# Attention and a routed expert layer in one kernel: expert 1's first weight sums one batch earlier, three x sums of the last third in the start-up of the expert units

## The chip, the cores and the metric

The kernel runs on one core of a Trainium2 chip. The metric is the time of one execution in microseconds; a change is judged by the median of several runs. The core's engines are TensorE (PE in the profile; PEld is its weight load), VectorE (DVE), ScalarE (ACT), GpSimd (POOL) and SyncE (SP). VectorE and ScalarE read and write SBUF and PSUM, GpSimd works on SBUF alone here. Each engine takes its own instructions in order and waits for other engines' semaphores.

## The reference

Block-sorted attention for 4 batches, 8 heads, 768 tokens of 64 values, followed by 8 experts whose outputs are all taken, weighted by a balanced routing matrix:

```python
P = sort_net                      # (4, 8, 8, 8); 5 rounds of exp and row/column normalisation
k_sorted = einsum('bhij,bhjcd->bhicd', P, k_b)      # blocks of 96 tokens; v_sorted alike
attn_out = softmax(q_b @ k_sb^T / 8) @ v_sb         # within each block
x = attn_out.transpose(0, 2, 1, 3).reshape(3072, 512)
P = exp(x @ w_gate - max)                           # (3072, 8); 8 rounds of row/column balancing
for e in range(8):
    out += P[:, e:e+1] * (relu(x @ w1[e]) @ w2[e])  # 512 -> 1024 -> 512
```

## The kernel before

**Attention, and expert 0 beside it.** The four batches go through the steps q (query transposes), k (sorted keys), s (scores), m (mixing with the values), t (transposes into xtT), l (routing logits). While batch bb runs, TensorE also computes expert 0 plainly for batch bb - 1 (`expert`: L299 first product, L306 second product). `weave` interleaves the two streams in a fixed order. The loop over bb runs from 1 to 3. In its middle stand the loads of the next batch's v, k and q (`load_batch`, L75, 768 KB each as bf16) and its sorting matrices (`build_r`, L140) on GpSimd, and then the sorting of the next batch's values (`sort_values`, TensorE L152, and sixteenths of the result moved by DMA at L161, half of them issued by GpSimd). In the last batch (bb = 3) this place holds `load_w1(1)` and the sums `sum_w(1)` (L332) instead. GpSimd also copies the queries of batches 2 and 3 (L179) ahead of their transposes.

**Experts 1 to 7.** These use Strassen-like 2x2 products (seven in place of eight), with sums of operands made beforehand. Per expert, `sum_w` makes sums of w1 (8 instructions on GpSimd), `sum_w2` sums of w2 (8 on GpSimd). For x there are three thirds of 1024 tokens; for each, `sum_x` makes four sums (L460): x1 = b12 - b11, x2 = b22 - x1, b12 = b22 - b12 in place, x4 = b21 - x2. The first third's are made by VectorE, unpinned; the second third's by GpSimd; the last third's by VectorE, one a unit from the second unit of chunk 1 on.

The work is cut into chunks (expert, third) of four units each; r counts the units. Unit r does seven first-layer products of chunk r // 4, p1, p5, p6, p2, p7, p3, p4 (`hidden`, L524), interleaved by position j with seven second-layer products q5 to q3 of a pair of token tiles five units back (`Pair`, L635). p7 and p3 end in a ReLU-and-add by VectorE (`relu_sum`, L513), p1, p5 and p6 in a copy by ScalarE, p2 and p4 in a ReLU by ScalarE (L510). p4 adds into the bank that p7's L513 reads. The second-layer banks are read by `gather` (L585, VectorE), which adds them with the routing weight into the output tiles osbl. Before a tile is first added to, `scale0` scales its part from expert 0 by the routing weight (L671, ScalarE). The operands hs of the second layer are made by GpSimd (`sums`, L625), one unit ahead. s (L575 by GpSimd in the first four units, L578 by VectorE later) is c11 - c12.

**The start-up** lies between attention and the units: `last_dense` (T; L692, L700, L704) computes expert 0 for batch 3, and `balance` (C) is the chain that balances the routing matrix: 26 steps, eight rounds of a row step (reduce, add, reciprocal), a column step (multiply, reduce L499) and a step with a matmul (L501) that sums over partitions and three VectorE operations. A string orders the two by hand; the rest of both runs in the first five units (r = 0 to 4), at positions j:

```python
dense, chain, xs = last_dense(), balance(), iter(())
for step in "TTCTTCTTCCTTCCTTTCTT":
    next({"T": dense, "C": chain}[step])
```

**What sets the order.** `pin` puts an instruction behind everything written before it on its engine. TensorE's matmuls are all pinned, and so are most instructions of the expert part. What isn't pinned is placed by a planner that works with costs of its own. `first_x` is a tiny GpSimd copy that reads the last of the first third's x sums; being pinned, it holds what GpSimd does next (expert 1's `sum_w2`, whose weights `load_w2(1)` fetches) until VectorE has made them. `weights(n)` issues n of the queued weight and x sums on GpSimd in each unit.

Of the kernel before, what the change touches and what calls it, by code (L numbers as in the profile page):

```python
# [14 lines left out]
BF16 = mybir.dt.bfloat16  # L15
# [10 lines left out]
def kernel(  # L26
# [11 lines left out]
    nc = tc.nc  # L38
# [25 lines left out]
    pin = tc.keep_in_program_order  # L64
    kt, vt, qt = {}, {}, {}

    def load_batch(bb, parts):
        for d, name in ((vt, "vt"), (kt, "kt"), (qt, "qt")):
            d[bb] = kvp.tile([128, 8, 384], BF16, name=name, bufs=2)
        load_rest(bb, parts)  # L70
# [11 lines left out]
    def load_w1(e):  # L82
        w1t[e] = wp.tile([128, 4, F], BF16, name="w1e")
        pin(nc.gpsimd.dma_start(out=w1t[e],
                                in_=moe_w1[e].rearrange("(kk k) f -> k kk f", k=128)))
# [238 lines left out]
    def sum_w(e):  # L324
        wct[e] = (wcq if e % 2 == 0 else wcp).tile([128, 3, 2, F // 2], BF16, name="wc")
        for kk in range(2):
            a11, a21 = (w1t[e][:, kk, f:f + 512] for f in (0, 512))
            a12, a22 = (w1t[e][:, 2 + kk, f:f + 512] for f in (0, 512))
            s1, s2, s4 = (wct[e][:, j, kk, :] for j in range(3))
            for a, b, o, c in ((a21, a22, ALU.add, s1), (s1, a11, ALU.subtract, s2),  # L330
                               (a11, a21, ALU.subtract, a21), (a12, s2, ALU.subtract, s4)):
                pin(nc.gpsimd.tensor_tensor(out=c, in0=a, in1=b, op=o))  # L332
                yield
# [46 lines left out]
    with ExitStack() as c2:  # L380
        pa = c2.enter_context(tc.tile_pool(name="pa", bufs=8, space=bass.MemoryType.PSUM,
                                           reuse_waits="tile"))
        bank1 = lambda shape, dt: pa.tile(shape, dt, name="bank", tag="bank")
        ebank = lambda: bank1([128, 512], F32)
        for bb in range(1, B):
            ex = expert0(bb - 1, lambda: mps.tile([128, 8, 384], BF16, name="hTs"),
                         ebank, ebank, pin)
            at1, left = attention(bb, bank1), 16 if bb == 1 else 26
            for _ in range(28 - left):
                next(ex)  # L390
            last = 3 if bb + 1 < B else 0
            left -= last
            cut = lambda k: left * k // 12
            weave(at1, ex, 5, cut(5))
            if bb + 1 < B:
                load_batch(bb + 1, [(x, 0, 8) for x in "vkq"])
                build_r(bb + 1, nc.gpsimd, 4)
            else:
                load_w1(1)
                sums = sum_w(1)  # L400
            weave(at1, ex, 3, cut(8) - cut(5))
            if bb + 1 < B:
                weave(sort_values(bb + 1, bank1), ex, 5, last)
            else:
                for _ in sums:
                    pass
            weave(at1, ex, 4, left - cut(8))
            for _ in ex:
                pass
# [6 lines left out]
    mpc, xcp, wq, wcq = late("mpc", 1), late("xcp", 1), late("wq", 2), late("wcq", 1)  # L416
# [36 lines left out]
    xc = xcp.tile([128, 3, 2, N // 2], BF16)  # L453

    def sum_x(p, eng, hold=pin):
        ta, tb = (slice(1024 * p + 512 * i, 1024 * p + 512 * i + 512) for i in range(2))
        b11, b12, b21, b22 = (xtT[:, k:k + 2, t] for k in (0, 2) for t in (ta, tb))
        x1, x2, x4 = (xc[:, j, :, 512 * p:512 * p + 512] for j in range(3))
        for a, b, c in ((b12, b11, x1), (b22, x1, x2), (b22, b12, b12), (b21, x2, x4)):
            hold(eng.tensor_tensor(out=c, in0=a, in1=b, op=ALU.subtract))  # L460
            yield

# [3 lines left out]
    nc.scalar.copy(I128, Ibig)  # L466
    for _ in sum_x(0, nc.vector, lambda ins: ins):
        pass
    first_x = mpc.tile([128, 2], BF16)
    pin(nc.gpsimd.tensor_copy(first_x, xc[:, 2, 0, 0:2]))  # L470

    def balance():

# [195 lines left out]
    def scale0(ts):  # L669
        for t in ts:  # L670
            pin(nc.scalar.activation(out=osbl[:, t, :], in_=osbl[:, t, :], func=AF.Copy,  # L671
                                     scale=glog[:, t, 0:1]))

    def last_dense():

        at = [0]

        def two_banks():
            at[0] += 1
            return rings["oacc"][at[0] % 2]  # L680

        for c in range(2):
            c0 = (B - 1) * S + c * 384
            if c == 0:
                h = [hTb[1][:, fb, 0:384] for fb in range(8)]
            else:
                two = [hsp.tile([128, 4, 384], BF16, name="hs") for _ in range(2)]
                h = [two[fb // 4][:, fb % 4, :] for fb in range(8)]
            for fb in range(8):
                hps = (rings["bk"][(0, 2, 3)[fb % 3]] if c == 0 else two_banks())[:, 0:384]  # L690
                for kk in range(4):
                    pin(nc.tensor.matmul(hps, w1t[0][:, kk, fb * 128:(fb + 1) * 128],  # L692
                                         xtT[:, kk, c0:c0 + 384],
                                         start=(kk == 0), stop=(kk == 3)))
                pin(relu(h[fb], hps))
                yield
            for tt in range(3):
                oacc = rings["bk"][(1, 4)[tt]] if c == 0 and tt < 2 else two_banks()
                for fb in range(8):
                    pin(nc.tensor.matmul(oacc, h[fb][:, tt * 128:(tt + 1) * 128],  # L700
                                         w2t[0][:, fb, :], start=(fb == 0), stop=(fb == 7)))
                    if fb == 3:
                        yield
                pin(nc.scalar.copy(osbl[:, c0 // 128 + tt, :], oacc))  # L704
                yield

    dense, chain, xs = last_dense(), balance(), iter(())
    for step in "TTCTTCTTCCTTCCTTTCTT":
        next({"T": dense, "C": chain}[step])

    queue = [sum_w2(1), sum_x(1, nc.gpsimd)]

    def weights(n):
# [6 lines left out]
    C = 3 * (E - 1)  # L720
# [4 lines left out]
    for m, o in enumerate(ends):  # L725
        e, p, hT, _ = chunks[-1]
# [4 lines left out]
    for r in range(len(pairs) + 6):  # L731
        n, i = r // 4, r % 4
        if n < C:
            e, p, hT, s3 = chunks[n]
            if i == 0 and (n == 1 or n > 1 and p == 0) and e + 1 < E:
                load_w1(e + 1)
                queue.append(sum_w(e + 1))
            if r == 8 or p == 1 and i == 2 and n > 1 and e + 1 < E:
                load_w2(2 if r == 8 else e + 1)
                queue.append(sum_w2(2 if r == 8 else e + 1))  # L740
            steps, rest = hidden(e, p, i, hT, s3, r < 4)
        else:
            steps, spares, rest = spares[:7], spares[7:], None
        if r == 5:
            xs = sum_x(2, nc.vector)
        k = r - 5
        if k + 1 in range(len(pairs)):
            pairs[k + 1].sums()
        weights((0, 2, 2, 0, 0)[r] if r < 5 else 4 if r < 8 else 1 + i % 2)
        now = pairs[k] if k in range(len(pairs)) else None  # L750
        if r < 5:
            outs = [lambda: next(dense), None, lambda: next(dense), None,
                    lambda: next(dense)]
        else:
            outs = [getattr(a, b) for a, b in
                    ((now, "q5"), (before, "q7"), (now, "q1"), (before, "q4"),
                     (now, "q6"), (now, "q2"), (now, "q3")) if a]
        if r == 5:
            for _ in chain:
                pass  # L760
            scale0([0, 4])
        for j in range(max(len(steps), len(outs))):
            if j < len(steps):
                steps[j]()
                if j == 3 and n < C:
                    if k + 1 in range(1, 12):
                        scale0([8 * ((k + 1) // 4) + (k + 1) % 4 + 4 * m for m in range(2)])
                    if k + 1 in range(len(pairs)):
                        pairs[k + 1].keep()
            if j < len(outs) and outs[j]:  # L770
                outs[j]()
            if r < 5 and j < 6 and (6 * r + j) % 4 != 3:
                next(chain, 0)
            if j == 1 and late:
                late()
                late = None
            if j == 3:
                next(xs, 0)
        late, before = rest, now
        if n >= C and not spares and not before:  # L780
            break
# [30 lines left out]
```

## Time and profile before

| | |
|---|---|
| median of 3 runs | 680.86 us (680.52 to 681.43) |
| profiled execution | 680.97 us, span 679.2 us |
| mean granted TensorE clock | 0.998 |
| TensorE busy | 659.0 us (97%) |
| VectorE busy | 474.8 us (70%) |
| ScalarE busy | 380.5 us (56%) |
| GpSimd busy | 473.6 us (70%) |

In the timeline a row gives the start, the time to the end of the group, the engine, the source line, the operation with its output and input tiles, and in brackets the idle time ahead of it and what ended it. In lists of waits the numbers are the total, the number of waits and the longest. In lists of DMA issues the last number is the time in us from issue to landing. Times are counted from the span's start.

The span falls into attention of batch 0 and its loads (0 to 49 us), attention of batches 1 to 3 with expert 0 beside it (49 to 135 us), the start-up (135 to 146 us) and the units (from 146 us).

### The profile page before, as it was taken

What the parts mean: (1) busy time and instruction counts of PE and PEld (TensorE: products, weight loads), DVE (VectorE), ACT (ScalarE), POOL (GpSimd) and SP (SyncE); (2) the same over time, 40 slices, a digit from 0 to 9 for tenths busy, and PEclk for the clock granted to TensorE, in tenths of its full rate; (3) what the DMA queues carried; (4) which work ended last, traced back from release to release, by engine and by line L of the source; (5) the groups of instructions that cost most, each with busy time, mean ns of one, the idle gap of its engine ahead of it and who ended that gap; (6) DMA issues with size and microseconds to landing.
All of it is one profiled execution on the core that took longest, in us unless ns stands there. A gap on an engine that the chain in (4) does not pass through costs nothing.

```text
span 679.2 us, 13352 instructions
## 1 busy us (share of the span) xinstructions
PE 659.0 (97%) x5136; PEld 434.1 (64%) x5136; DVE 474.8 (70%) x977; ACT 380.5 (56%) x737; POOL 473.6 (70%) x439
## 2 busy tenths in 40 slices
PE   4989999999999999999999999999999999999997
PEld 2656666554566666666666666666666666666665
DVE  6727556758587777777777777777777777777775
ACT  3757646356767765455555555555555555555540
POOL 4542324474979998959697988879796979836641
PEclk9999999999999999999999999999999999999999
DMA  9898843402140304030403030020303040000224
GB/s 146 168 217 127 139 82 63 63 1 37 28 62 2 63 1 63 1 63 1 63 1 63 1 50 14 12 52 3 61 1 63 1 63 1 1 0 32 94 84 167
DMA packets 31905, 36.58 MB, mean 54 GB/s; under 512 B 2016, under 2 KB 24288, under 8 KB 31840
## 3 DMA queue, kind: packets, MB, share of 16 engines
q0 software_dynamic: 26400, 27.82, 25.8%
q1 hardware_dynamic: 5440, 7.90, 3.4%
q8 instruction: 40, 0.66, 0.4%
q14 instruction: 25, 0.20, 0.1%
HBM read 52.45 MB, written 6.29 MB: 86 GB/s over the span
## 4 chain that ended last, share of the span: by engine, by line
PE 88%; DVE 5%; DMA 4%; issue 1%; ACT 1%; POOL 1%; SPq 0%; DVEq 0%; POOLq 0%
PE oacc L635 36%; PE bk L524 36%; PE bank L299 4%; PE bank L306 3%; DMA qt<-in_q_dram 3%; PE bank L232 1%; PE bk L601 1%; PE oacc L700 1%; PE bk L692 1%; DMA vsb<-vs 1%; PE bank L215 1%; PE bank L196 1%; PE bank L243 1%; DVE xc L460 1%; PE bk L700 1%
## 5 line engine op out<-in xcount | busy, mean ns | idle before, releaser
L585 DVE SCALAR_TENSOR_TENSOR osbl<-oacc,glog,osbl 128x256 f32<-128x256 f32 (+1 forms) x410 | 219.4, 536 | 127.7 <-PE oacc L635 117.8
L510 ACT ACTIVATE hT<-bk 128x512 bf16<-128x512 f32 (+1 forms) x176 | 104.2, 592 | 151.8 <-PE bk L524 131.9
L524 PE MATMUL bk<-xtT,w1e 128*128 128x512 bf16 x504 | 149.1, 379 | 0.0
L635 PEld LDWEIGHTS <-hs 128*128 128x128 bf16 x984 | 96.3, 98 | 63.0 <-issue 0.3
L635 PEld LDWEIGHTS <-hT 128*128 128x128 bf16 x904 | 88.4, 98 | 59.6 <-issue 2.4
L625 POOL TENSOR_TENSOR hs<-hT 128x512 bf16<-128x512 bf16 x82 | 94.7, 1155 | 38.3 <-DVE hT L513 28.6
L635 PE MATMUL oacc<-w2e,hT 128*128 128x256 bf16 x764 | 114.6, 273 | 1.1 <-DVE osbl L585 1.1
L625 POOL TENSOR_TENSOR hs<-hT,hs 128x512 bf16<-128x512 bf16 x82 | 95.1, 1159 | 6.4
L625 POOL TENSOR_TENSOR hs<-hs,hT 128x512 bf16<-128x512 bf16 x82 | 95.1, 1159 | 6.4
L524 PE MATMUL bk<-xc,wc 128*128 128x512 bf16 x336 | 99.1, 379 | 0.0
L635 PE MATMUL oacc<-w2e,hs 128*128 128x256 bf16 x616 | 92.4, 273 | 0.0
L524 PEld LDWEIGHTS <-w1e 128*128 128x128 bf16 x672 | 65.7, 98 | 14.9 <-issue 3.6
L559 ACT COPY p<-bk 128x512 f32<-128x512 f32 x84 | 49.1, 585 | 23.9 <-PE bk L524 23.8
L513 DVE CUSTOM_DVE_ANT_0 hT<-bk,p 128x512 bf16<-128x512 f32 x84 | 57.9, 690 | 6.6 <-PE bk L524 1.9
L553 ACT COPY u<-bk 128x512 f32<-128x512 f32 x84 | 49.2, 586 | 22.2 <-PE bk L524 22.1
L544 ACT COPY bk<-bk 128x512 f32<-128x512 f32 x84 | 48.0, 571 | 20.5 <-PE bk L524 20.5
L513 DVE CUSTOM_DVE_ANT_0 hT<-bk,u 128x512 bf16<-128x512 f32 x84 | 57.2, 681 | 0.6 <-PE bk L524 0.6
L635 PE MATMUL oacc<-w2s,hs 128*128 128x256 bf16 x368 | 55.2, 273 | 0.0
L578 DVE SCALAR_TENSOR_TENSOR s<-bk,hT 128x512 bf16<-128x512 f32 x80 | 54.5, 681 | 0.0
L524 PEld LDWEIGHTS <-wc 128*128 128x128 bf16 x504 | 49.4, 99 | 7.5
L524 PE MATMUL bk<-xc,w1e 128*128 128x512 bf16 x168 | 49.9, 379 | 1.9 <-DVE hT L513 1.8
L524 PE MATMUL bk<-xtT,wc 128*128 128x512 bf16 x168 | 50.0, 379 | 0.0
(129 smaller groups left out, 858.5 us busy)
## 6 DMA issues: line engine op xcount, KB each, us to landing
w1e<-in_moe_w_dram POOLq DMA_DIRECT2D x8, 1024.0 KB, 8.1
w2e<-in_moe_w_dram POOLq DMA_DIRECT2D x8, 1024.0 KB, 8.9
out_dram<-osbl SPq DMA_DIRECT2D x23, 256.0 KB, 2.0
vt<-in_v_dram POOLq DMA_DIRECT2D x3, 768.0 KB, 10.5
vsb<-vs SPq DMA_DIRECT2D x16, 97.5 KB, 4.8
vsb<-vs POOLq DMA_DIRECT2D x16, 97.5 KB, 4.4
qt<-in_q_dram POOLq DMA_DIRECT2D x4, 384.0 KB, 12.8
kt<-in_k_dram POOLq DMA_DIRECT2D x4, 384.0 KB, 13.3
```

The source lines that it names most:

```text
L299: hold(nc.tensor.matmul(hps[:, 0:n], w1t[e][:, kk, fb * 128:(fb + 1) * 128], xtT[:, kk, c0:c0 + n], start=(kk == 0), stop=(kk == 3)))
L306: hold(nc.tensor.matmul(oacc, hTs[:, fb, tt * 128:(tt + 1) * 128], w2t[e][:, fb, :], start=(fb == 0), stop=(fb == 7)))
L510: relu = lambda o, x: nc.scalar.activation(out=o, in_=x, func=AF.Relu)
L513: return nc.vector._custom_dve(TENSOR_ADD_SAT, out=o, in0=x, in1=y, s0=TOP, s1=0.0)
L524: pin(nc.tensor.matmul(ps, wa[:, kk, :], xa[:, kk, :], start=(first and kk == 0), stop=(kk == 1), skip_group_check=True))
L544: pin(nc.scalar.copy(t["w"], t["u"]))
L553: pin(nc.scalar.copy(t["u2"], t["u"]))
L559: pin(nc.scalar.copy(t["p5"], t["v"]))
L578: pin(nc.vector.scalar_tensor_tensor(out=s3[:, i, :], in0=t["w"], scalar=0.0, in1=c12, op0=ALU.max, op1=ALU.subtract))
L585: pin(nc.vector.scalar_tensor_tensor(out=o, in0=ps, scalar=glog[:, t, e:e + 1], in1=o, op0=ALU.mult, op1=ALU.add))
L625: pin(nc.gpsimd.tensor_tensor(out=s[:, c], in0=a, in1=b, op=o))
L635: pin(nc.tensor.matmul(ps, h[:, fb, :], w[:, fb, :], start=(first and fb == 0), stop=(fb == 3), skip_group_check=True))
```

## The change

`load_w1(1)` moves from the middle of bb = 3 to that of bb = 2, ahead of the loads for batch 3; `sum_w(1)` follows there, behind `build_r`. In `sum_x` the last two sums change places, so that x4 is the third and the sum in place the fourth. `first_x` goes. Three of the last third's sums (X) are written into the start-up's string, and a tiny GpSimd copy, `held_x`, waits for the third of them. The fourth is issued once, at the end of the third unit of chunk 1 (r = 6, j = 6). The scaling of output tiles 0 and 4 moves from the head of unit 5 into unit 4 (at j = 2 and j = 5). The slots of the balancing chain in the first units move from j = 0 to 5 to j = 0, 1, 2, 4, 5, 6, with the same ones left out.

```diff
--- before.py
+++ after.py
@@ -393,17 +393,16 @@
             cut = lambda k: left * k // 12
             weave(at1, ex, 5, cut(5))
             if bb + 1 < B:
+                if bb == 2:
+                    load_w1(1)
                 load_batch(bb + 1, [(x, 0, 8) for x in "vkq"])
                 build_r(bb + 1, nc.gpsimd, 4)
-            else:
-                load_w1(1)
-                sums = sum_w(1)
+                if bb == 2:
+                    for _ in sum_w(1):
+                        pass
             weave(at1, ex, 3, cut(8) - cut(5))
             if bb + 1 < B:
                 weave(sort_values(bb + 1, bank1), ex, 5, last)
-            else:
-                for _ in sums:
-                    pass
             weave(at1, ex, 4, left - cut(8))
             for _ in ex:
                 pass
@@ -456,7 +455,7 @@
         ta, tb = (slice(1024 * p + 512 * i, 1024 * p + 512 * i + 512) for i in range(2))
         b11, b12, b21, b22 = (xtT[:, k:k + 2, t] for k in (0, 2) for t in (ta, tb))
         x1, x2, x4 = (xc[:, j, :, 512 * p:512 * p + 512] for j in range(3))
-        for a, b, c in ((b12, b11, x1), (b22, x1, x2), (b22, b12, b12), (b21, x2, x4)):
+        for a, b, c in ((b12, b11, x1), (b22, x1, x2), (b21, x2, x4), (b22, b12, b12)):
             hold(eng.tensor_tensor(out=c, in0=a, in1=b, op=ALU.subtract))
             yield
 
@@ -466,8 +465,6 @@
     nc.scalar.copy(I128, Ibig)
     for _ in sum_x(0, nc.vector, lambda ins: ins):
         pass
-    first_x = mpc.tile([128, 2], BF16)
-    pin(nc.gpsimd.tensor_copy(first_x, xc[:, 2, 0, 0:2]))
 
     def balance():
 
@@ -704,9 +701,11 @@
                 pin(nc.scalar.copy(osbl[:, c0 // 128 + tt, :], oacc))
                 yield
 
-    dense, chain, xs = last_dense(), balance(), iter(())
-    for step in "TTCTTCTTCCTTCCTTTCTT":
-        next({"T": dense, "C": chain}[step])
+    dense, chain, xs = last_dense(), balance(), sum_x(2, nc.vector)
+    for step in "TTCXTTCXTTCCXTTCCTTTCTT":
+        next({"T": dense, "C": chain, "X": xs}[step])
+    held_x = mpc.tile([128, 2], BF16)
+    pin(nc.gpsimd.tensor_copy(held_x, xc[:, 2, 0, 1024:1026]))
 
     queue = [sum_w2(1), sum_x(1, nc.gpsimd)]
 
@@ -741,8 +740,6 @@
             steps, rest = hidden(e, p, i, hT, s3, r < 4)
         else:
             steps, spares, rest = spares[:7], spares[7:], None
-        if r == 5:
-            xs = sum_x(2, nc.vector)
         k = r - 5
         if k + 1 in range(len(pairs)):
             pairs[k + 1].sums()
@@ -758,7 +755,6 @@
         if r == 5:
             for _ in chain:
                 pass
-            scale0([0, 4])
         for j in range(max(len(steps), len(outs))):
             if j < len(steps):
                 steps[j]()
@@ -769,13 +765,15 @@
                         pairs[k + 1].keep()
             if j < len(outs) and outs[j]:
                 outs[j]()
-            if r < 5 and j < 6 and (6 * r + j) % 4 != 3:
+            if r < 5 and j != 3 and (6 * r + j - (j > 3)) % 4 != 3:
                 next(chain, 0)
+            if r == 4 and j in (2, 5):
+                scale0([4 if j == 2 else 0])
             if j == 1 and late:
                 late()
                 late = None
-            if j == 3:
-                next(xs, 0)
+            if r == 6 and j == 6:
+                next(xs)
         late, before = rest, now
         if n >= C and not spares and not before:
             break
```

## The prediction

> **What bounds the kernel now.** I read the list of engines first: TensorE is busy in all but the first slices, and the clock row shows it at full rate. So only time in which TensorE stands still can be won here, and the next view is the list of waits of TensorE, cut to the stretch from 150 to 200 us, where the first expert units run.
>
> ```profile
> PE bk L524 <- DVE hT L513: 1.8, 5, 0.6
> PE oacc L635 <- DVE osbl L585: 1.1, 1, 1.1
> ```
>
> Five waits are for a VectorE ReLU-and-add (L513), one is for an output accumulation (L585). Before 150 us there is one more place, in the last batch of attention. TensorE's timeline there:
>
> ```profile
> 119.58 0.81 PE L299 MATMUL bank<-xtT,w1e 128*128 128x384 bf16 x4
> 120.87 0.20 PE L215 MATMUL bank<-qTs,kTs 64*96 64x96 bf16 x1 [0.48 <-DVE osbl L314]
> ...
> 122.62 1.47 PE L299 MATMUL bank<-xtT,w1e 128*128 128x384 bf16 x8
> ```
>
> And the same sixteen score matmuls one batch earlier, without a stop:
>
> ```profile
> 86.27 0.56 PE L215 MATMUL bank<-qTs,kTs 64*96 64x96 bf16 x16
> ```
>
> From 119.58 to 122.62 are 3.04 us. The four L299 matmuls take 1.47 - 0.81 = 0.66 (eight less four), the sixteen L215 take 0.56. So 1.8 us are lost, more than the single waits of the list show.
>
> What was VectorE doing? The x sums of the first third (L460). Two groups over the whole run, with minimum/median/maximum in ns and the first and last start, and one of the timeline:
>
> ```profile
> L460 DVE TENSOR_TENSOR xc<-xtT,xc x4: 677/884/1456, 117.2 to 199.0; 128x1024 bf16<-128x1024 bf16 x4
> L460 DVE TENSOR_TENSOR xc<-xtT x2: 1318/1476/1635, 115.8 to 179.3; 128x1024 bf16<-128x1024 bf16 x2
> ```
> ```profile
> 118.57 1.64 DVE L460 TENSOR_TENSOR xtT<-xtT 128x1024 bf16<-128x1024 bf16 x1
> ```
>
> The same operation costs 0.68 or up to 1.64. The three in the last batch took 1.32 (at 115.8), 1.46 (the first group's longest, at 117.2) and 1.64; the one at 179.3 took 1.64 too. The slow ones run while GpSimd does expert 1's first weight sums, which read and write SBUF too. Behind them stand the copies that free PSUM banks (L314), and TensorE waits for those.
>
> **Part 1: expert 1's first weights, one batch sooner.** In the last batch GpSimd then has no sums, so the x sums of the first third should cost 0.68 each. The three give VectorE back 1.32 + 1.46 + 1.64 - 3 x 0.68 = 2.4 us ahead of the L314 that TensorE waited for, and its score matmuls begin only 0.63 (1.29 less 0.66) after they could. I count the whole 1.8 us as won.
>
> The price is paid at 73 us. The load of w1 (1 MB) goes into GpSimd's queue and into the DMA queue ahead of the three loads for batch 3; behind these the eight sums, and behind the sums the query copies (L179) and half of the value stores (L161) of batch 3. The loads, each with its time to landing; the load of w1 as it runs alone, one batch later; GpSimd's issue of vt; TensorE's first use of it:
>
> ```profile
> vt<-in_v_dram POOLq DMA_DIRECT2D x1, 768.0 KB, 7.3
> kt<-in_k_dram POOLq DMA_DIRECT2D x1, 768.0 KB, 10.9
> qt<-in_q_dram POOLq DMA_DIRECT2D x1, 768.0 KB, 13.9
> ```
> ```profile
> w1e<-in_moe_w_dram POOLq DMA_DIRECT2D x1, 1024.0 KB, 8.3
> ```
> ```profile
> 73.23 0.92 POOL L75 DMA_DIRECT2D vt<-in_v_dram  x1
> ```
> ```profile
> 90.63 0.49 PE L152 MATMUL bank<-vt,R 128*128 128x384 bf16 x2
> ```
>
> In queue order w1 lands at 73.2 + 8.3 = 81.5 and vt at the latest 7.3 later, at 88.8; needed at 90.63. So vt costs nothing by 1.8 us, and this is the nearest of the covers: beyond it each further microsecond is lost on TensorE. The keys and queries are used in batch 3's attention, which begins when all its values are sorted, and they land at most 8.3 later than now. Eight sums of 1.15 run from 81.5 to about 91, before the queries have landed, so nothing queued behind them is held by them. Cost 0 (to 5.7, the rival below).
>
> **Part 2: three x sums of the last third in the start-up, GpSimd held.** Before, these sums sat at the start of the second unit and in later ones (179 to 199 us). Now they stand on VectorE between the first steps of the balancing chain (135 to 146 us), 3 x 0.68 = 2.0 us. The chain has room there:
>
> ```profile
> 147.59 0.17 DVE L502 TENSOR_SCALAR cs<-oacc 128x8 f32<-128x8 f32 x1 [3.20 <-PE oacc L501]
> ```
>
> VectorE waits 3.20 us for a chain matmul that TensorE reaches late in its order, so 2.0 more is hidden. Before that, one chain matmul follows VectorE closely; the third sum comes behind its input but the second lies ahead: I take 0.1 lost, 0 to 0.3.
>
> The tiny copy that waits for the third of these sums holds GpSimd's queue: behind it are expert 1's second weight sums, the x sums of the second third, and the four s differences (L575). Their start, and the idle time in front of the four:
>
> ```profile
> 134.81 1.14 POOL L450 TENSOR_TENSOR w2s<-w2e 128x512 bf16<-128x512 bf16 x1 [8.42 <-DMA w2e<-in_moe_w_dram]
> ```
> ```profile
> L575 POOL TENSOR_TENSOR s<-hT 128x512 bf16<-128x512 bf16 x4 | 4.6, 1153 | 8.9 <-DVE hT L513 4.5 <-ACT hT L510 4.4
> ```
>
> The third sum is done between 142 and 144 (VectorE ran dry at 147.59 - 3.20 = 144.4). GpSimd thus starts 7 to 9 us later and has 8.9 us of idle time to make up. Its results are first used after 170 us. Cost 0.
>
> **Part 3: the units.** The gaps of the second and third unit (start to start):
>
> ```profile
> 180.39 0.59 PE L524 MATMUL bk<-xtT,wc 128*128 128x512 bf16 x2
> 181.55 0.59 PE L524 MATMUL bk<-xc,w1e 128*128 128x512 bf16 x2 [0.56 <-DVE hT L513]
> ...
> 186.75 0.60 PE L635 MATMUL oacc<-w2e,hT 128*128 128x256 bf16 x4
> 187.79 0.59 PE L524 MATMUL bk<-xc,w1e 128*128 128x512 bf16 x2 [0.44 <-DVE hT L513]
> ```
> ```profile
> 156.01 0.59 PE L524 MATMUL bk<-xtT,wc 128*128 128x512 bf16 x2
> 157.04 0.59 PE L524 MATMUL bk<-xc,w1e 128*128 128x512 bf16 x2 [0.43 <-DVE hT L513]
> 157.47 0.59 PE L524 MATMUL bk<-xtT,w1e 128*128 128x512 bf16 x2
> 157.90 0.81 PE L692 MATMUL oacc<-xtT,w1e 128*128 128x384 bf16 x4
> 158.55 0.28 PE L501 MATMUL oacc<-cs,onesc 128*128 128x8 f32 x2
> ```
>
> Two matmuls back to back take 0.43 (157.04 to 157.47). So 180.39 to 181.55 loses 0.73, 186.75 to 187.79 loses 0.61. Each has an x sum ahead of the L513 (the 1.64 at 179.3 before the first); without it I count 0.65 (the ReLU-and-add of 0.68 still only just fits its two groups of 0.43) and 0.6. Smaller waits at the last two moved sums I leave uncounted.
>
> The fourth sum, b22 - b12 in place, now comes at the end of the third unit, with GpSimd at work beside it. Nothing in the trace shows it there. Bounds: 0, and 0.73, the largest gap a slowed sum made. It stands behind the unit's last accumulation and not straight ahead of an L513, so I take 0.3. The Trainium skill, SBUF — State Buffer, section "Who interferes with whom", says that an operation with both inputs in SBUF and a GpSimd operation that reads SBUF exclude each other for the whole instruction. By that rule the sum takes 0.68 plus a wait of 0 to 1.15, as the 0.68 and 1.64 agree, and an estimate of its cost by the mean would be nearer 0.4.
>
> The scaling of output tiles 4 and 0 moves from the head of the second unit into the first chunk's last unit. Before:
>
> ```profile
> 175.46 0.59 PE L524 MATMUL bk<-xc,wc 128*128 128x512 bf16 x2
> 177.18 0.60 PE L635 MATMUL oacc<-w2e,hT 128*128 128x256 bf16 x4 [1.12 <-DVE osbl L585]
> ```
> ```profile
> 176.64 0.48 DVE L585 SCALAR_TENSOR_TENSOR osbl<-oacc,glog,osbl 128x256 f32<-128x256 f32 x1 [1.49 <-ACT osbl L671]
> ```
>
> 1.72 less 0.43 is 1.29 lost: ScalarE scales, VectorE accumulates (0.48), TensorE goes on into the same bank. With the scaling done sooner the accumulation starts 0.16 behind its matmuls (0.59 less 0.43) and takes 0.48, against 0.43 of cover: 0.2 to 0.3 stays. Gain 1.0.
>
> Last, the chain's slots move from j = 3, 4, 5 to 4, 5, 6, so that a step no longer stands ahead of the L513 that TensorE waits for at 157.04 (gap 1.03 - 0.43 = 0.60). But the steps then pile up behind it. VectorE there:
>
> ```profile
> 155.52 0.37 DVE L494 TENSOR_REDUCE oacc<-oacc 128x24 f32<-128x192 f32 x1
> ...
> 156.36 0.63 DVE L513 CUSTOM_DVE_ANT_0 hT<-bk,p 128x512 bf16<-128x512 f32 x1
> 156.90 0.35 DVE L498 TENSOR_TENSOR oacc<-oacc,rs 128x192 f32<-128x192 f32 x1
> 157.29 0.36 DVE L499 TENSOR_REDUCE cs<-oacc 128x8 f32<-128x192 f32 x1
> ```
>
> A row step costs 0.84 (155.52 to 156.36), a column step 0.75. After the change: L513 from about 155.5, row step to 157.05, second L513 to 157.65, column step to 158.4. The chain's matmul (L501), which TensorE now reaches at 158.55 - 0.60 = 157.95, waits for that until 158.45. So 0.1 of the 0.60 is kept. The fourth unit has the same pattern with a smaller wait, of which I count 0.2. Together 0.3, between 0 and 0.9.
>
> **The sum.** 1.8 - 0.1 + 0.3 + 1.0 + 0.65 + 0.6 - 0.3 = 3.95 us. The profiled execution took 680.97 us, 0.11 above the median of the three runs; its span is 679.2. From the median: 680.86 - 3.95 = 676.9. A run cannot tell less than 0.2% (1.4 us) from no change.
>
> One limit lies behind it. GpSimd works almost without a pause from 170 us until it waits for expert 2's second weights:
>
> ```profile
> 204.42 1.16 POOL L450 TENSOR_TENSOR w2e<-w2e 128x512 bf16<-128x512 bf16 x1 [3.72 <-DMA w2e<-in_moe_w_dram]
> 205.53 1.16 POOL L625 TENSOR_TENSOR hs<-hT 128x512 bf16<-128x512 bf16 x1
> ```
> ```profile
> 207.72 0.60 PE L635 MATMUL oacc<-w2s,hs 128*128 128x256 bf16 x4
> ```
>
> hs is ready at 206.69 and used at 207.72: 1.0 us of slack. GpSimd itself comes forward by about 1.5 (an estimate: it had to wait out up to 0.68 for each of three sums of VectorE that are gone), TensorE by 2.25 inside the units. It fits with little to spare, so a larger gain in the units would be cut off here.
>
> **The rivals.**
>
> *The order is not what the text says (0.12).* The first third's sums and the copies around them are not pinned; the planner may put the three sums ahead of L314 with another neighbour behind them, or keep the bank copies late. Then the 1.8 stays: 680.86 - 2.15 = 678.7. For it: they start where the buffers come free, whatever else waits. Against: the wait is explained by the sums' length alone.
>
> *The units give it back (0.10).* VectorE has little room in the first units, and the chain's matmul and the fourth sum could eat all that parts 2 and 3 win except the 1.0 of the scaling: 1.8 + 1.0 - 0.8 = 2.0, so 678.9.
>
> *The loads share the DMA engines (0.05), the slower side.* If w1, vt, kt and qt went side by side, vt would land with the last of them, up to 73.2 + 8.3 + 13.9 = 95.4 or, with issue times, 96.3: TensorE would stand 5.7 us at 90.63, against 3.95 won: 682.6. It decides from a landing of vt after 94.6. Against it: the three landed at 7.3, 10.9 and 13.9, one behind the other. The Trainium skill, DMA: Bandwidth & Descriptors, section "Queues, rings and completion order", has an engine share its time between queues, and take one queue's descriptors in order; the three landings agree.
>
> *GpSimd is late (0.07).* If the load of expert 1's second weights came behind the held copy, its sums would begin 8.4 after 143, near 151.6 and not 142 to 144. GpSimd would be some 3.6 us late at 170 (after all idle time), 2 at 205.53, and hs would come at about 209 for a use at 207.72: 682.2 at worst, about no change if half of it is made up.
>
> **How the numbers follow.** The forecast, 676.9, has 0.66. The bounds of its terms reach from 675.5 (all gaps of the units closed, the fourth sum free) to 678.2. With the first two rivals the range goes to 678.9. Faster by over 0.2%: 0.86. Within 0.2%: 0.08, the late GpSimd mostly. Slower: 0.06.
>
> **What would show it.** In the changed trace the first third's x sums take 0.68 and the sixteen L215 of batch 3 run without a stop; L332 for expert 1 begins near 81.5; no wait at vt; three VectorE L460 lie before 145 us; L585 no longer waits for L671; a new short wait of L501 for L499 appears near 156. Wrong it would be if L152 waits for vt, if the bank wait at L215 stays above 1 us, or if waits for hs on GpSimd appear between 190 and 210 us.

## The result and the profile after

The changed kernel takes 677.71 us (median of 4 runs, 677.30 to 677.94) against 681.11 us (680.52 to 681.43). The ratio is 0.9948, with a 95% interval of 0.9936 to 0.9960: 3.4 us faster, where 3.95 were forecast (as a time, 676.9). In a later set of runs it was 677.58 against 681.52, ratio 0.9943 (0.9929 to 0.9958).

The list of waits of TensorE over the whole changed execution, in the columns that the prediction used:

```profile
PE bank L174 <- DMA qt<-in_q_dram: 9.7, 3, 7.7
PE oacc L632 <- DVE osbl L582: 1.1, 2, 0.8
PE bank L352 <- DVE Prep L128: 0.6, 1, 0.6
PE bank L306 <- DMA w2e<-in_moe_w_dram: 0.5, 1, 0.5
PE bank L152 <- DMA vt<-in_v_dram: 0.5, 1, 0.5
PE bank L257 <- ACT xtT L246: 0.4, 1, 0.4
PE oacc L498 <- DVE cs L496: 0.3, 1, 0.3
PE bank L232 <- ACT atp L222: 0.3, 1, 0.3
```

The waits for the ReLU-and-add (now L510) are gone from it, and so are those of L215. One for the chain (L498) is new. Of the two waits for an accumulation (L632), one of 0.3 lies behind the fourth sum (below); the one of 0.8 comes after 250 us, and the kernel before has it too. The waits for transfers all lie in the first 50 us, where nothing was changed.

The last batch in the changed kernel's timelines, VectorE and then TensorE (start in us and duration of each group):

```profile
116.69 0.67 DVE L459 TENSOR_TENSOR xc<-xtT 128x1024 bf16<-128x1024 bf16 x1
117.46 0.69 DVE L459 TENSOR_TENSOR xc<-xtT,xc 128x1024 bf16<-128x1024 bf16 x1
118.07 0.68 DVE L459 TENSOR_TENSOR xtT<-xtT 128x1024 bf16<-128x1024 bf16 x1
118.67 0.68 DVE L314 COPY osbl<-bank 128x512 f32<-128x512 f32 x1
```
```profile
120.49 0.81 PE L299 MATMUL bank<-xtT,w1e 128*128 128x384 bf16 x4
121.23 0.56 PE L215 MATMUL bank<-qTs,kTs 64*96 64x96 bf16 x16
121.72 1.47 PE L299 MATMUL bank<-xtT,w1e 128*128 128x384 bf16 x8
```

The order on VectorE is the one from before, the same three sums ahead of the same copy. Only their lengths differ, and the sixteen score matmuls run through: 1.23 us from L299 to L299 in place of 3.04.

The price at 73 us: the DMA view's four loads in the order of their issue (w1 at 74.1, vt at 74.9; last the us from issue to landing), and the first use of vt in the timeline of TensorE:

```profile
w1e<-in_moe_w_dram POOLq DMA_DIRECT2D x1, 1024.0 KB, 9.6
vt<-in_v_dram POOLq DMA_DIRECT2D x1, 768.0 KB, 12.2
kt<-in_k_dram POOLq DMA_DIRECT2D x1, 768.0 KB, 15.2
qt<-in_q_dram POOLq DMA_DIRECT2D x1, 768.0 KB, 18.1
```
```profile
91.54 0.49 PE L152 MATMUL bank<-vt,R 128*128 128x384 bf16 x2
```

They land one behind the other, although w1, the first in the queue, took 9.6 us and not the 8.3 that it took alone. vt is there at 74.9 + 12.2 = 87.1, 4.4 us ahead of its use.

The places that the prediction priced in the units: the chain's new wait, the second unit, and the fourth sum with the matmul behind it, in the changed kernel's timelines (TensorE twice, VectorE, TensorE):

```profile
157.66 0.39 PE L498 MATMUL oacc<-cs,onesc 128*128 128x8 f32 x2 [0.32 <-DVE cs L496]
```
```profile
174.04 0.60 PE L632 MATMUL oacc<-w2s,hs 128*128 128x256 bf16 x4
174.69 0.59 PE L521 MATMUL bk<-xc,wc 128*128 128x512 bf16 x2
175.28 0.60 PE L632 MATMUL oacc<-w2e,hT 128*128 128x256 bf16 x4
```
```profile
186.48 1.28 DVE L459 TENSOR_TENSOR xtT<-xtT 128x1024 bf16<-128x1024 bf16 x1
187.69 0.86 DVE L582 SCALAR_TENSOR_TENSOR osbl<-oacc,glog,osbl 128x256 f32<-128x256 f32 x2
```
```profile
188.21 0.60 PE L632 MATMUL oacc<-w2e,hT 128*128 128x256 bf16 x4 [0.27 <-DVE osbl L582]
```

### The profile page after: what moved, and what is told of

Its sections match the earlier page's. It is cut to its first block, busy times and chain, and to the rows that moved or that the text cites. A ratio compares the mean times of both kernels' runs of the same rounds, so it can differ in the third digit from the quotient of the medians.

```text
span 676.1 us, 13351 instructions
## 1 busy us (share of the span) xinstructions
PE 658.7 (97%) x5136; PEld 433.8 (64%) x5136; DVE 471.7 (70%) x977; ACT 380.3 (56%) x737; POOL 470.3 (70%) x439
## 4 chain that ended last, share of the span: by engine, by line
PE 91%; DMA 4%; DVE 3%; POOL 1%; ACT 1%; issue 0%; SPq 0%; DVEq 0%; POOLq 0%
PE oacc L632 37%; PE bk L521 37%; PE bank L306 4%; PE bank L299 4%; DMA qt<-in_q_dram 3%; PE bank L232 1%; PE bk L598 1%; PE oacc L697 1%; DMA vsb<-vs 1%; PE bk L689 1%; PE bank L215 1%; PE bank L196 1%; PE bank L243 1%; PE bk L697 1%; PE oacc L689 0%; PE bank L183 0%
## 5 line engine op out<-in xcount | busy, mean ns | idle before, releaser
L632 PEld LDWEIGHTS <-hs 128*128 128x128 bf16 x984 | 96.3, 98 | 63.0 <-issue 0.3
L632 PEld LDWEIGHTS <-hT 128*128 128x128 bf16 x904 | 88.4, 98 | 58.9 <-issue 1.8
L632 PE MATMUL oacc<-w2e,hT 128*128 128x256 bf16 x764 | 114.6, 273 | 0.3 <-DVE osbl L582 0.3
L632 PE MATMUL oacc<-w2e,hs 128*128 128x256 bf16 x616 | 92.4, 273 | 0.0
L510 DVE CUSTOM_DVE_ANT_0 hT<-bk,p 128x512 bf16<-128x512 f32 x84 | 58.1, 692 | 7.8 <-PE bk L521 3.1
L510 DVE CUSTOM_DVE_ANT_0 hT<-bk,u 128x512 bf16<-128x512 f32 x84 | 57.1, 680 | 1.0 <-PE bk L521 0.6
L632 PE MATMUL oacc<-w2s,hs 128*128 128x256 bf16 x368 | 55.2, 273 | 0.0
## 6 DMA issues: line engine op xcount, KB each, us to landing
vt<-in_v_dram POOLq DMA_DIRECT2D x3, 768.0 KB, 12.2
```

The costliest lines, as they stand in the source:

```text
L510: return nc.vector._custom_dve(TENSOR_ADD_SAT, out=o, in0=x, in1=y, s0=TOP, s1=0.0)
L632: pin(nc.tensor.matmul(ps, h[:, fb, :], w[:, fb, :], start=(first and fb == 0), stop=(fb == 3), skip_group_check=True))
```

## The experiments

To see terms of tenths of a microsecond, I compare stretches of TensorE's timeline between the same matmuls of each kernel, and only from 72 us on: the query transposes (L183) of batch 2, the chain's first matmul (L481 before, L478 after), the first q5 of the units, the matmul that reads the spare tile near 200 us, and the end of the span. Up to the first of these nothing differs between the kernels. In us:

| kernel | first L183 | to chain | to q5 | to spare | to end | sum |
|---|---|---|---|---|---|---|
| before | 71.06 | 65.75 | 38.21 | 29.23 | 474.95 | 608.14 |
| changed | 71.97 | 63.94 | 38.13 | 27.19 | 474.87 | 604.13 |
| changed, again | 71.27 | 63.94 | 38.13 | 27.21 | 474.95 | 604.23 |
| w1_only | 71.51 | 63.93 | 38.15 | 29.23 | 474.98 | 606.29 |
| scale_only | 71.49 | 65.87 | 38.21 | 28.85 | 475.08 | 608.01 |
| chain_only | 71.94 | 65.74 | 38.15 | 28.93 | 474.94 | 607.76 |
| xs_only | 71.41 | 65.63 | 38.22 | 27.68 | 474.96 | 606.49 |
| no_hold | 71.52 | 63.94 | 38.13 | 27.19 | 474.92 | 604.18 |
| fourth_r5 | 71.67 | 63.94 | 38.14 | 26.76 | 475.29 | 604.13 |
| fourth_r8 | 71.66 | 63.93 | 38.13 | 26.76 | 474.92 | 603.74 |
| fourth_r8_warm | 71.54 | 63.94 | 38.14 | 26.76 | 475.02 | 603.86 |
| head_fourth | 71.41 | 63.93 | 39.29 | 26.77 | 475.50 | 605.49 |
| head_fourth_r8 | 72.02 | 63.94 | 39.31 | 26.76 | 474.87 | 604.88 |

The first column spreads over 1 us without any change behind it, and the profiled execution of before was the luckiest of the thirteen. The other columns repeat within 0.1 to 0.2 where the kernels do not differ. From L183 to the end the change gains 608.14 - 604.13 = 4.0 us.

**w1_only** is the kernel before with the first part alone.

```diff
+                if bb == 2:
+                    load_w1(1)
                 load_batch(bb + 1, [(x, 0, 8) for x in "vkq"])
                 build_r(bb + 1, nc.gpsimd, 4)
-            else:
-                load_w1(1)
-                sums = sum_w(1)
+                if bb == 2:
+                    for _ in sum_w(1):
+                        pass
...
-            else:
-                for _ in sums:
-                    pass
```

> The kernel before with part 1 alone: the load and the sums of expert 1's first weights in the batch before; the order of the x sums and the first hold stay. Theory (VectorE's x sums and GpSimd's weight sums keep each other out, and TensorE pays in the last batch): the three sums of the first third take 0.68 us each, the sixteen L215 run without a stop, the time falls by 1.8 us, ratio 0.9974. Rival (the order of the banks' copies in the last batch makes the wait, whatever the sums take): the sums get shorter, at least 1 us of the wait at L215 stays, under 0.8 us is won.

679.72 against 681.33 us, ratio 0.9973 (0.9964 to 0.9983). The column to the chain falls by 1.82, all others stay. The wait at L215 goes although the order of the copies is untouched. The three sums take 0.67, 0.69 and 0.69. That is the theory's result to the tenth in the trace; the medians differ by 1.6.

**scale_only** moves the scaling of tiles 4 and 0 alone.

```diff
-            scale0([0, 4])
...
+            if r == 4 and j in (2, 5):
+                scale0([4 if j == 2 else 0])
```

> The kernel before with the scaling of output tiles 0 and 4 moved into the unit before, nothing else. Theory: q1 of the second unit waits 0.2 to 0.3 in place of 1.1 us (1.29 by the starts), 0.9 to 1.0 us are won. Rival (the wait is the accumulation's, not the scaling's): L585 still ends late, under 0.4 us is won.

681.19 against 681.33, ratio 0.9992 (0.9980 to 1.0004): by the time alone this can't be told from nothing. In the trace q1 comes 1.24 us behind q5 in place of 2.16, so the 0.92 at that place are won as expected. At the spare tile 0.38 is left in all. Here the x sums still stand in the units: two of them got shorter (1.64 to 1.25 and 1.09 to 0.97), which won 0.42 more, and the third got longer, which lost 0.96 (the timelines of this kernel, VectorE, GpSimd, then TensorE):

```profile
191.94 1.64 DVE L460 TENSOR_TENSOR xtT<-xtT 128x1024 bf16<-128x1024 bf16 x1
```
```profile
191.88 1.16 POOL L625 TENSOR_TENSOR hs<-hT 128x512 bf16<-128x512 bf16 x1
```
```profile
194.24 0.59 PE L524 MATMUL bk<-xc,w1e 128*128 128x512 bf16 x2 [1.00 <-DVE hT L513]
```

In the kernel before, the same sum took 0.68, but it met GpSimd there too, and it was GpSimd's operation that grew from 1.15 to 1.63 (timelines of before, VectorE, then GpSimd):

```profile
192.73 0.68 DVE L460 TENSOR_TENSOR xtT<-xtT 128x1024 bf16<-128x1024 bf16 x1
```
```profile
192.80 1.63 POOL L625 TENSOR_TENSOR hs<-hs,hT 128x512 bf16<-128x512 bf16 x1
```

Before, VectorE began 0.07 us sooner and GpSimd's operation was long; here GpSimd began 0.06 us sooner and VectorE's sum was long. So a gain ahead of these sums shifts the phase between the two engines, and with it, by these rows, which of them pays. This is a result that neither theory had.

**chain_only** moves the chain's slots alone.

```diff
-            if r < 5 and j < 6 and (6 * r + j) % 4 != 3:
+            if r < 5 and j != 3 and (6 * r + j - (j > 3)) % 4 != 3:
```

> The kernel before with the slots of the balancing chain moved alone (j = 3, 4, 5 to 4, 5, 6). Theory: the waits of p4 for L513 near 157 and 168 go, and the chain's matmul L501 waits about as long instead; 0.1 us won, 0 to 0.3. Rival (the chain has slack and the waits of p4 are simply gone): 0.9 to 1.0 us won (0.60 and 0.38), no wait at L501.

680.84 against 681.33, ratio 0.9993 (0.9984 to 1.0002), by the time alone not told from nothing. Up to q5 the trace gains 0.06, and L501 waits for L499 as the theory has it. The 0.30 between q5 and the spare tile are again a shift of phase at the x sums: the one at 180.07 took 1.33 in place of 1.64. The rival's 0.9 is out.

**xs_only** moves the x sums and the hold alone.

```diff
-        for a, b, c in ((b12, b11, x1), (b22, x1, x2), (b22, b12, b12), (b21, x2, x4)):
+        for a, b, c in ((b12, b11, x1), (b22, x1, x2), (b21, x2, x4), (b22, b12, b12)):
...
-    dense, chain, xs = last_dense(), balance(), iter(())
-    for step in "TTCTTCTTCCTTCCTTTCTT":
-        next({"T": dense, "C": chain}[step])
+    dense, chain, xs = last_dense(), balance(), sum_x(2, nc.vector)
+    for step in "TTCXTTCXTTCCXTTCCTTTCTT":
+        next({"T": dense, "C": chain, "X": xs}[step])
+    held_x = mpc.tile([128, 2], BF16)
+    pin(nc.gpsimd.tensor_copy(held_x, xc[:, 2, 0, 1024:1026]))
...
-        if r == 5:
-            xs = sum_x(2, nc.vector)
...
-            if j == 3:
-                next(xs, 0)
+            if r == 6 and j == 6:
+                next(xs)
```

> The kernel before with the x sums alone: x4 third, three of the last third's sums in the start-up, GpSimd held for them, the fourth at the end of the third unit. Expert 1's first weight sums stay in the last batch. Theory: the gaps at L513 in the second to fifth unit (0.73, 0.61, 0.2, 0.2) go down to 0.1 in all, the fourth sum costs 0.4: 1.1 to 1.3 us won. Rival (TensorE is held at q5 by the scaling in that unit anyway and the sums had been hidden): under 0.5 us won. A second rival (GpSimd, held until 141, is late with its sums): waits for GpSimd from 175 us on, no gain.

679.82 against 681.33, ratio 0.9979 (0.9970 to 0.9987), and 1.65 us in the trace, 1.55 of them from q5 to the spare tile. That is more than expected, because the fourth sum took 0.68 here (at 188.61) and cost nothing. It met GpSimd all the same: GpSimd's weight sum at 188.68 took 1.62 in place of 1.15. The start-up lost nothing to the three sums (to q5: 38.22 against 38.21). No wait for GpSimd appeared.

The four parts, from L183 on, gain 1.85 + 0.13 + 0.38 + 1.65 = 4.0, as much as the whole. That it comes out so closely is partly luck, since scale_only and chain_only hold gains and losses of phase at x sums that the changed kernel no longer has in the units. Between q5 and the spare tile alone the parts give 0.38 + 0.30 + 1.55 = 2.23 and the whole 2.04.

**no_hold** takes the held copy out of the changed kernel. It ran twice.

```diff
-    held_x = mpc.tile([128, 2], BF16)
-    pin(nc.gpsimd.tensor_copy(held_x, xc[:, 2, 0, 1024:1026]))
```

> The changed kernel without the tiny copy that holds GpSimd: expert 1's second weight sums and the x sums of the second third run as soon as their data are there, beside VectorE's three x sums of the start-up. Theory (the two engines keep each other out for whole instructions): GpSimd's sums of 1.15 and 2.12 us lie at 125 to 143; the three x sums take 0.68 plus waits of up to 2.1, 1.2 to 2.7 each; the chain's matmul L498, which came without a wait at 140.54, waits 1 to 3 us: 1 to 3 us slower than the changed kernel, 678.7 to 680.7. Rival (VectorE has 3.2 us of slack in the start-up, the hold is worth nothing): the sums are long, the time is within 0.4 us of the changed kernel.

> The changed kernel without the held copy, once more, for a profile. Its times so far lay at 677.2 to 678.1, within 0.3 us of the changed kernel. Theory of the lock: the x sums of the start-up overlap GpSimd's sums and are long, TensorE waits for L496 near 140; this costs 1 to 3 us, which the times speak against. Rival: VectorE's slack of 3.2 us takes the long sums; the chain's matmul at 140.5 comes without a wait. Third: the chain's matmul waits some tenths, and GpSimd, which is done sooner, gives as much back at hs.

677.70 in the first set; 677.53 in the second, where the changed kernel took 677.58. By these and by the sums of the table (604.18 against 604.13 and 604.23) the hold is worth nothing, and the theory's 1 to 3 us are wrong. The timelines of VectorE and GpSimd in the start-up without it, from the second of its profiles (the row of the table is of that one too):

```profile
136.08 0.67 DVE L459 TENSOR_TENSOR xc<-xtT 128x1024 bf16<-128x1024 bf16 x1
137.66 0.68 DVE L459 TENSOR_TENSOR xc<-xtT,xc 128x1024 bf16<-128x1024 bf16 x1
139.93 1.09 DVE L459 TENSOR_TENSOR xc<-xtT,xc 128x1024 bf16<-128x1024 bf16 x1
```
```profile
136.20 1.57 POOL L449 TENSOR_TENSOR w2s<-w2e,w2s 128x512 bf16<-128x512 bf16 x1
137.73 1.63 POOL L449 TENSOR_TENSOR w2s<-w2e 128x512 bf16<-128x512 bf16 x1
139.32 1.15 POOL L449 TENSOR_TENSOR w2s<-w2e,w2s 128x512 bf16<-128x512 bf16 x1
140.43 2.56 POOL L459 TENSOR_TENSOR xc<-xtT 128x1024 bf16<-128x1024 bf16 x1
```

The two do keep each other out, but at the first two sums GpSimd paid (1.57 and 1.63 for 1.15), since VectorE began just as GpSimd's sum ended. The third sum waited 0.4, behind the step that the chain's matmul needs, and GpSimd's next one took 2.56 in place of 2.12. VectorE's idle time in front of the next chain step took the 0.4: it was 2.76 us here and 3.17 in the changed kernel. With another phase it could cost something; that wasn't seen.

**fourth_r5** puts the fourth x sum of the changed kernel where VectorE stood idle.

```diff
-            if r == 6 and j == 6:
+            if r == 5 and j == 1:
                 next(xs)
```

> The changed kernel with the fourth x sum of the last third one unit sooner, at r = 5, j = 1, where VectorE stood idle for 1.2 us. Theory (the 0.43 at q1 of the unit at 188 is the wait of its accumulation for this sum): that wait goes, no new one over 0.2; 0.4 us won against the changed kernel as far as GpSimd keeps up: its hs for the unit at 204.7 were ready only 0.2 us ahead of use in the changed kernel, so 0.2 to 0.4. Rival (the wait is the lock's and comes wherever the sum stands): the same 0.4 at another matmul.

677.65 us, with the first no_hold at 677.70 in the same set. The sum was not shorter in its new place: it ran at 175.45 for 1.53 us, but in VectorE's idle time. In the trace the 0.43 at q1 goes (to spare: 26.76 against 27.19), and 0.4 comes back behind it (475.29 against 474.87), at a wait for GpSimd (the timelines of this kernel, TensorE, then GpSimd):

```profile
204.40 0.61 PE L632 MATMUL oacc<-w2s,hs 128*128 128x256 bf16 x4 [0.25 <-POOL hs L622]
```
```profile
202.08 1.16 POOL L449 TENSOR_TENSOR w2e<-w2e 128x512 bf16<-128x512 bf16 x1 [4.41 <-DMA w2e<-in_moe_w_dram]
203.19 1.15 POOL L622 TENSOR_TENSOR hs<-hT 128x512 bf16<-128x512 bf16 x1
```

This is the limit that the prediction named. GpSimd idles 4.41 us for a load with the next hs queued behind it.

**fourth_r8** is fourth_r5 and takes that weight sum out of the way as well.

```diff
-    weights((0, 2, 2, 0, 0)[r] if r < 5 else 4 if r < 8 else 1 + i % 2)
+    weights((0, 2, 2, 0, 0)[r] if r < 5 else 4 if r < 8 else 0 if r == 8 else 1 + i % 2)
```

> The changed kernel with the fourth sum at r = 5, j = 1, and no weight sum at r = 8 behind the load of expert 2's second weights. Theory: the 0.43 at the sum is won and the 0.2 that TensorE then waited for hs near 204 goes too: 128.65 from the first query copy to the spare tile, 0.6 us under the changed kernel. Rival (GpSimd's limit moves on to the next hs): a wait of 0.2 or more for hs later than 204.

677.13 us, where the changed kernel took 677.58 in the same set. GpSimd's hs now runs while the load is under way (the timeline of GpSimd in this kernel):

```profile
197.65 1.15 POOL L622 TENSOR_TENSOR hs<-hT 128x512 bf16<-128x512 bf16 x1
198.88 1.16 POOL L622 TENSOR_TENSOR hs<-hs,hT 128x512 bf16<-128x512 bf16 x1
200.11 1.16 POOL L622 TENSOR_TENSOR hs<-hT,hs 128x512 bf16<-128x512 bf16 x1
202.06 2.39 POOL L449 TENSOR_TENSOR w2e<-w2e 128x512 bf16<-128x512 bf16 x2 [0.80 <-DMA w2e<-in_moe_w_dram]
```

The wait for hs is gone and the sum falls to 603.74, 0.4 to 0.5 below the changed kernel. Its ratio to before, 0.9936 (0.9923 to 0.9949), overlaps that of the changed kernel, so by the time it is better by its median only; by the trace the 0.4 has a place.

**head_fourth** (with the edit of fourth_r5) and **head_fourth_r8** (with that of fourth_r8) put three more chain steps into the start-up, and with them other slots are left out in the units.

```diff
-    for step in "TTCXTTCXTTCCXTTCCTTTCTT":
+    for step in "TTCXTTCXTTCCXTTCCTTTCTCCCT":
...
-            if r < 5 and j != 3 and (6 * r + j - (j > 3)) % 4 != 3:
+            if r < 5 and j != 3 and (6 * r + j - (j > 3)) % 4 != 0:
```

> The changed kernel with the fourth sum at r = 5, j = 1, and three more steps of the balancing chain in the start-up, so that it ends about one round sooner (slots % 4 != 0). Theory (in the first four units VectorE is full, and the waits for L498 and L510 there, 0.35 at 150.4, 0.1 at 153.5, 0.6 at 157.7 and 0.1 at 169, are its backlog): VectorE works in the 3.2 us that it stood idle from 143.5, these waits fall to 0.4 in all, 0.8 us won up to q5 of r = 5; but GpSimd's hs then come late near 203, so the total gains 0.2 to 0.6 against the changed kernel, with a new wait for GpSimd there. Rival (GpSimd has room): no such wait, 1.2 us won. Second rival (the chain's new matmul in the start-up makes TensorE wait there): a wait for L496 at 144 to 147, nothing won.

> As head_fourth, and at r = 8 GpSimd is not given the first sum of expert 2's second weights right behind their load (it waits for the load there, 4.2 us, with the next hs queued behind it). Theory (that queue is the limit for whatever is won in the units): hs comes 3 us or more ahead of its use at r = 10, no wait for GpSimd; 1.0 to 1.2 us won against the changed kernel, 676.5. Rival (nothing was limited there): the same time as head_fourth within 0.2.

678.93 and 678.44 us, slower than the changed kernel's 677.6: the stretch to q5 grew from 38.13 to 39.3. VectorE did work earlier, but the chain's matmuls fell to other places, and TensorE waited for them there. Whether the earlier steps or the shifted slots did it was not separated. The largest wait, from the timeline of TensorE in head_fourth_r8:

```profile
159.33 0.39 PE L498 MATMUL oacc<-cs,onesc 128*128 128x8 f32 x2 [0.72 <-DVE cs L496]
```

The second rival holds in its kind, a wait for L496, though the large one is in the units and not at 144 to 147. GpSimd's limit shows here too: 0.6 between the two kernels in the column to the end.

**fourth_r8_warm** adds to fourth_r8 one tiny ReLU-and-add at 143 us.

```diff
+    first = mpc.tile([128, 2], BF16)
+    pin(relu_sum(first, I128[:, 0:2], I128[:, 0:2]))
```

> As fourth_r8, with one tiny ReLU-and-add (128x2) on VectorE in its idle time at 143 us, so that the first one of the units isn't the kernel's first. Theory (the first ReLU-and-add starts 0.4 to 0.6 us after its inputs because VectorE meets that operation for the first time): in the unit at 145 it starts within 0.1 us of its inputs and the 0.35 us that p4 waits near 150 go. Rival (it waits for something else, as the profile's varying releasers say): the tiny one has no delay of its own and the 0.35 stays.

677.23 us, no gain. The tiny operation and the first one of the units, in this kernel's timeline of VectorE:

```profile
143.01 0.27 DVE L510 CUSTOM_DVE_ANT_0 first<-I 128x2 bf16<-128x2 f32 x1
```
```profile
149.18 0.69 DVE L510 CUSTOM_DVE_ANT_0 hT<-bk,p 128x512 bf16<-128x512 f32 x1 [0.37 <-POOL w2s L449]
```

The tiny one follows its neighbour at once, and the 0.37 ahead of the first large one stays. So it isn't the first use. The releaser that the profile infers changes from kernel to kernel, and what it waits for stays open.

## Why the prediction was right, point by point

**The last batch**: 1.8 forecast, 1.81 in the column to the chain, 1.82 with this part alone. Reading the loss from the starts (3.04 against 0.66 + 0.56) and not from the listed waits (1.1) was what sized it. Its cover held: vt had 4.4 us to spare where I had bounded it by 1.8. Two steps went otherwise at no cost. The first weight sum began at 83.82 and not 81.5, since w1 was issued at 74.14 and took 9.6. And I had the eight sums end at 91, before the queries; the planner put a query copy between them (the changed kernel's timeline of GpSimd):

```profile
94.96 0.82 POOL L179 COPY qr<-qt 128x768 bf16<-128x768 bf16 x1 [5.42 <-PE bank L299]
```

The last three sums waited behind it and the value stores went out from 99.8 on; TensorE's list of waits has none between 50 and 150 us.

One reading was incomplete. I took the long sums as those that run beside GpSimd and the 0.68 as a sum by itself. But the fourth sum of the first third took 0.68 before, at 123.55, while GpSimd was at its weight sums as well; that time GpSimd's was the long one (timelines of before, VectorE, then GpSimd):

```profile
123.55 0.68 DVE L460 TENSOR_TENSOR xc<-xtT,xc 128x1024 bf16<-128x1024 bf16 x1
```
```profile
123.52 1.72 POOL L332 TENSOR_TENSOR wc<-w1e,wc 128x512 bf16<-128x512 bf16 x1
```

These two starts lie too close together to say which came first. This part of the forecast did not suffer, because with the weight sums gone GpSimd had no operation left there to meet.

**The start-up**: 0.1 forecast, 0.0 measured (the stretch from the chain's first matmul to the matmul near 147 is 10.46 in both). GpSimd started its sums at 141.31 and had made it up by 162.50, where it idled again.

**The chain's slots**: 0.3 forecast, 0.08 measured up to q5, the term of those counted that was mis-sized most. The step itself was right: the wait moves from L510 to L498. By the starts, 0.60 is won at the second unit's last matmul and 0.59 lost at the L498 behind it (157.66), where I had 0.1 kept. In the fourth unit 0.38 is won and 0.16 lost at 169.05, so 0.22 is kept, the 0.2 of the forecast. What I had not counted is the chain's matmul one round earlier. In the kernel before and in the changed one:

```profile
153.71 0.81 PE L692 MATMUL oacc<-xtT,w1e 128*128 128x384 bf16 x4
154.36 0.29 PE L501 MATMUL oacc<-cs,onesc 128*128 128x8 f32 x2
154.50 1.02 PE L524 MATMUL bk<-xtT,w1e 128*128 128x512 bf16 x4
```
```profile
152.74 0.81 PE L689 MATMUL oacc<-xtT,w1e 128*128 128x384 bf16 x4
153.47 0.39 PE L498 MATMUL oacc<-cs,onesc 128*128 128x8 f32 x2
153.72 1.02 PE L521 MATMUL bk<-xtT,w1e 128*128 128x512 bf16 x4
```

From the first row to the last are 0.79 before and 0.98 after: 0.19 lost. The first unit wins 0.07.

**The second unit**: 1.0 and 0.65 forecast, 0.92 and 0.55 measured. **The third unit**: 0.6 and 0.60. The gaps that I left uncounted, at the last two sums, gave 0.2 each.

**The fourth sum**: 0.3 forecast, 0.43 measured in the changed kernel, 0 in xs_only. In both it met GpSimd's weight sums; in the changed kernel GpSimd's had begun first, at 186.06, and the sum at 186.48 took 1.28, while in xs_only VectorE was first by 0.07. So 0.3 stood for a phase that I did not know, and that it lies near the 0.43 is luck. The estimate by the Trainium skill's rule (SBUF — State Buffer, "Who interferes with whom") was nearer 0.4; two cases do not tell the one from the other. What the rule says of the mechanism agrees: 0.68 without a wait, 1.28 with one.

Together 1.81 + 0.08 + 0.92 + 0.55 + 0.60 - 0.43 + 0.4 = 3.93, where 3.95 were forecast. So close a sum is luck: the chain, the second unit and the fourth sum came out worse by 0.2, 0.2 and 0.1, and the start-up and the gaps left out made up for it by 0.1 and 0.4. The medians of the first set differ by 3.4, half a microsecond less. In the two profiled executions (680.97 and 677.94) the changed kernel stands 0.91 later at 72 us, ahead of the change, and in the later set, with other runs of before, the difference was 3.9 us (681.52 to 677.58). That the half microsecond lies there in the other executions too is likely, but no trace shows it.

**The rivals.** The order was as the text says (w1_only). The loads landed in queue order. GpSimd was not late for the units in the changed kernel, since the load of expert 1's second weights was issued at 115.86, long ahead of the hold; but it stood 0.2 from being the limit, as fourth_r5 and fourth_r8 show. The units gave back 0.43 at the fourth sum and most of what the moved slots won at L510, both of which were priced, if not to the tenth.

## What to carry to other kernels

Price a stall from start to start against an undisturbed copy of the same work, not from the listed waits, and look for an operation that has two durations: here the longer one named a neighbour on another engine. Look at the neighbour's durations as well, since a short one on this side can be a long one over there. Parts that look alike in value need not be worth their place alone: moving the scaling bought 0.92 us at one matmul, and 0.38 of it was left as long as VectorE's sums still met GpSimd by chance of phase. When TensorE comes forward, look at the queue whose head waits for a load, and let work that is ready pass it.

## What the runs showed that I had not expected

The copy that holds GpSimd for three sums, part of the change's purpose, was worth nothing: without it the sums took 0.67, 0.68 and 1.09 us, and GpSimd paid at each of the meetings, by 0.4 to 0.5 us. In three meetings of a sum of VectorE with an operation of GpSimd (192.73 before, 191.94 in scale_only, 188.61 in xs_only) the one that began first, by less than 0.1 us, was the short one and the other the long one. And executions of any of these kernels differ by up to 1 us in the first 72 us (71.06 to 72.02 in thirteen profiles), a quarter of what was to be measured.
